# GpSimd adds the 1e-9 to the softmax row sums, and two engines share the last output copy: an attention, gate and bilinear chain on one core

## The chip, the cores and the metric

The kernel runs on one core of a Trainium2 chip. The metric is the device time of one execution in microseconds (us). Engines are named as in the profile: PE is TensorE (PEld its weight loads), DVE is VectorE, ACT is ScalarE, POOL is GpSimd, SP issues the DMAs.

## What is computed

Causal attention over 2 batches, 12 heads, 448 tokens, head size 64, then two dense layers in float32:

```python
scores = np.where(mask, -1e9, (q @ k^T) / sqrt(64))
attn = exp(scores - max); attn = attn / (attn.sum(-1) + 1e-09)
x = (attn @ v) as 896 x 768
h = x @ w_in;  y = (h * cos(h)) @ w_out
out = ((y @ w_a) * (y @ w_b)) @ w_o2
```

## The kernel before

The two heads of a pair lie on the two halves of the 128 partitions, so there are 12 pairs n = 0 to 11. The seven 64-token blocks j of queries of a pair fall into two halves: the even blocks 6, 0, 4, 2 and the odd blocks 5, 3, 1. Below, En and On are the even and the odd half of pair n. For each half the work goes through all engines in turn:

- `scores` (L339): PE multiplies q and k into four PSUM banks.
- `row_max` (L362): DVE adds the mask, takes the row minimum of the negated scores and writes them into one of two buffers p.
- `exps` (L383): ACT takes the exponentials in place and writes each block's row sums into one column of a small tile `sums`, 128x4 for En, 128x3 for On.
- `recip` (L388): DVE adds 1e-9 to that tile (L390) and takes its reciprocal (L391).
- `scale_p` (L398): POOL multiplies the four or three pieces of p by the reciprocals.
- `transposes` (L412): PE transposes seven 128x128 pieces of p into two PSUM banks `pt`, four into the first, three into the second.
- `keep` (L423, L425): one bank is copied to `pp` by ACT, the other by DVE.
- `values` (L439): PE multiplies `pp` and v; `x_hi`, `x_lo` (L449, L454) split the result into a high and a low part.

Every engine runs its instructions strictly in the order in which they were written, and that order is set by hand: a loop over steps i, in each of which the table `CYCLE` is gone through. A pair takes four steps. `(recip, 2, 0)` puts the reciprocal of En at step 4n+2 and `(scale_p, 3, 0)` its scaling at 4n+3; for On they are at 4n+4 and 4n+5. On DVE the next thing behind a `recip` is in most steps a `keep` copy, whose bank the next transposes on PE need.

Beside this, weights are fetched and split into high and low parts (`w_scale`, `w_shift`, `w_pack`, `w_sign`, `w_hi`, `w_lo`); `ASIDE` and `PUMPS` place these by step, behind the entries of `CYCLE`. For the first three chunks both `w_hi` (L129) and `w_lo` (L138) are POOL's; chunk 0 is at step 28, chunk 1 at step 39. From step 44 on, pieces of the first dense layer (L175) fill PE between the attention's parts.

After about 85 us the dense layers follow, with three matmuls per product (high times high, high times low, low times high). At the end each of the 12 output blocks is copied from PSUM by DVE into a tile `o` (L568) and sent off by a DMA from SP's queue (L569).

```python
        CYCLE = [(row_max, 0), (scores, -2), (recip, 2, 0), (recip, 4, 1),
            (keep, 6, 0), (keep, 8, 1), (exps, 0), (scale_p, 3, 0), (scale_p, 5, 1), ...]
```

Of the kernel before, what the change touches and what calls it, by code (L numbers as in the profile page):

```python
# [12 lines left out]
ACTF = mybir.ActivationFunctionType  # L13
ALU = mybir.AluOpType
# [12 lines left out]
def tile_causal_attention_cos_gate_bilinear(  # L27
# [16 lines left out]
    nc = tc.nc  # L44
    B, NPAIR = qk.shape[:2]
    D = P // 2
    S = out.shape[1] // B
    NP = B * NPAIR
    NJ = S // D
    N_IN, N_Y, N_C = w_in.shape[0], w_out.shape[0], w_a.shape[0]  # L50
# [12 lines left out]
    def act_tiles(pool, tag, kind, b, n):  # L63
        return [
            tuple(pool.tile([P, S], F32R, tag=f"{tag}{b}_{t}{part}", name=f"{kind}{b}_{t}{part}") for part in ("hi", "lo"))
            for t in range(n)
        ]
# [73 lines left out]
    def w_pump():  # L141

        i, odd = divmod(next(pumps), 2)
        if odd:
            w_shift(i)
            w_pack(i)
        else:
            w_sign(i - 1)
            w_hi(i - 1)
            w_lo(i - 1, nc.gpsimd)  # L150
            w_scale(i)

    def split(src, pair, lo_engine=None):
        nc.scalar.activation(pair[0], src, ACTF.Copy)
        (lo_engine or nc.vector).tensor_tensor(out=pair[1], in0=src, in1=f32(pair[0]), op=ALU.subtract)
# [10 lines left out]
    def product(kind, f, acts, name, release, parts=1):  # L166

        ps = bank(next(cycle), name)[:, :S]
        n = len(acts)
        t = j = 0  # L170
        while t < n:
            hi, lo, k = chunks[kind, f, j]
            terms = [(hi, c, part) for c in range(k) for part in range(2)] + [(lo, c, 0) for c in range(k)]
            for i, (w, c, part) in enumerate(terms):
                nc.tensor.matmul(  # L175
                    ps,
                    w[:, c * P : (c + 1) * P],
                    acts[t + c][part],
                    start=t == 0 and i == 0,
                    stop=t + k == n and i == len(terms) - 1,  # L180
                )
                if (i + 1) % (len(terms) // parts) == 0 and i + 1 < len(terms):
                    yield ps
            t += k
            if release:
                del chunks[kind, f, j]
            if kind != "in":
                w_pump()
            j += 1
        yield ps  # L190
# [7 lines left out]
    def rows(u):  # L198
        if u < len(units):
            f, b = units[u]  # L200
            stages[u] = next(product("in", f, x[b], "h", b == B - 1))
# [7 lines left out]
    def turns(u):  # L209
        if u in stages:  # L210
            ps = stages[u]
            k = work.tile([P, S], I32, tag="k", name="k", bufs=1)
            r = work.tile([P, S], F32, tag="r", name="r")
            nc.scalar.activation(k, ps, ACTF.Copy, scale=1.0 / TWO_PI)  # L214
            nc.vector.scalar_tensor_tensor(out=r, in0=k, scalar=-TWO_PI, in1=ps, op0=ALU.mult, op1=ALU.add)  # L215
            stages[u] = (ps, r)

    def sine(u):
        if u in stages:
            r = stages[u][1]  # L220
            nc.scalar.activation(r, r, ACTF.Sin, scale=0.5)  # L221

    def square(u):
        if u in stages:
            r = stages[u][1]
            nc.scalar.activation(r, r, ACTF.Square, scale=2.0**0.5)  # L226

    def gate(u):
        if u in stages:
            ps, r = stages[u]  # L230
            nc.vector.scalar_tensor_tensor(out=r, in0=r, scalar=1.0, in1=ps, op0=ALU.subtract, op1=ALU.mult)  # L231

    def g_out(u):
        if u in stages:
            f, b = units[u]
            split(stages.pop(u)[1], g[b][f], nc.gpsimd)
# [23 lines left out]
    P_OFF, o = {}, 0  # L260
# [18 lines left out]
    with ExitStack() as actx:  # L279
# [6 lines left out]
        for o in (0, S):  # L286
            for e in range(2):
                half = mask[e * D : (e + 1) * D, o : o + D]
                nc.gpsimd.affine_select(
                    out=half,  # L290
# [96 lines left out]
        @pairs  # L387
        def recip(n, odd):  # L388
            t = T["sums", n, odd][:, : NB - odd]
            nc.vector.tensor_scalar_add(t, t, 1e-9)  # L390
            nc.vector.reciprocal(t, t)  # L391

        @pairs
# [69 lines left out]
        def at(fn, i):  # L463
# [6 lines left out]
            (row_max, 0),  # L470
            (scores, -2),
            (recip, 2, 0),
            (recip, 4, 1),
            (keep, 6, 0),
            (keep, 8, 1),
# [49 lines left out]
    with tc.manual_schedule():  # L525
        g = [act_tiles(g_pool, "g", "g", b, N_IN) for b in range(B)]
        for u in range(EARLY):
            gate(u - 2)
            turns(u)
            sine(u - 1)  # L530
            g_out(u - 2)
            square(u - 1)
            if u < EARLY - 1:
                w_pump()
        for u in range(EARLY, len(units) + 2):
            gate(u - 2)
            rows(u)
            turns(u)
            sine(u - 1)
            g_out(u - 2)  # L540
            square(u - 1)
            w_pump()


        y = [act_tiles(xy, "xy", "y", b, N_Y) for b in range(B)]
        for m in range(N_Y):
            for b in range(B):
                ps = next(product("out", m, g[b], "y", b == B - 1))
                split(ps, y[b][m])


        c = [act_tiles(g_pool, "g", "c", b, N_C) for b in range(B)]
        for f in range(N_C):
            for b in range(B):
                ps_b = next(product("b", f, y[b], "b", b == B - 1))
                bs = work.tile([P, S], F32, tag="k", name="bs", bufs=1)
                nc.scalar.activation(bs, ps_b, ACTF.Copy)
                ps_a = next(product("a", f, y[b], "a", b == B - 1))
                c32 = work.tile([P, S], F32, tag="r", name="c32")
                nc.vector.tensor_tensor(out=c32, in0=ps_a, in1=bs, op=ALU.mult)  # L560
                split(c32, c[b][f])


        for m in range(N_Y):
            for b in range(B):
                ps = next(product("o2", m, c[b], "o", b == B - 1))
                o = work.tile([P, S], F32, tag="r", name="o")
                nc.vector.tensor_copy(o, ps)  # L568
                nc.sync.dma_start(out=out[m * P : (m + 1) * P, b * S : (b + 1) * S], in_=o)  # L569


# [46 lines left out]
```

## Time and profile before

| | |
|---|---|
| median of 3 runs | 583.26 us (582.53 to 583.45) |
| the profiled execution | 582.98 us, its span 581.2 us |
| PE busy | 572.7 us, 99% of the span |
| DVE, ACT, POOL busy | 360.5, 267.3, 222.7 us |
| granted TensorE clock | 1.0 throughout |

The span runs from the first to the last instruction on the engines; 1.8 us of the profiled execution lie around it. Busy shares are averages over stages with different limits: attention fills the first 85 us of the span and the dense layers the rest. A busy PE is not PE at its peak, since matmuls are pipelined and their ends are modelled.

### The profile page before, as it was taken

How to read it: one execution, taken by the hardware profiler on the slowest of the kernel's cores; microseconds unless marked ns; L12 is line 12 of the kernel's file. 1: busy time of each engine (PE TensorE's matmuls, PEld its weight loads, DVE VectorE, ACT ScalarE, POOL GpSimd, SP SyncE). 2: the span in 40 equal slices, each digit the busy share in tenths (PEclk: the TensorE clock that was granted, in tenths of full speed). 3: DMA queues.
4: the chain of work that ended last, by engine and by line, in shares of the span. 5: the costliest groups of instructions: out<-in, count | busy, mean ns of one | idle time of the engine just before them, and what ended most of it. 6: DMA issues, size and time to landing. Idle time of an engine off the chain costs nothing.

```text
span 581.2 us, 8736 instructions
## 1 busy us (share of the span) xinstructions
PE 572.7 (99%) x3310; PEld 512.1 (88%) x3310; DVE 360.5 (62%) x599; ACT 267.3 (46%) x531; POOL 222.7 (38%) x200
## 2 busy tenths in 40 slices
PE   8999999999999999999999999999999999999997
PEld 6666679999999999999999999999999999999996
DVE  5788856777777775554465666666666666655400
ACT  5877947777777733232223433333333333222100
POOL 4557752666666643232222322222222222322200
PEclk9999999999999999999999999999999999999999
DMA  8745311333332333423243333333323333444000
GB/s 322 264 150 192 109 57 55 109 109 109 109 109 92 108 116 122 144 91 109 91 162 109 110 109 109 108 109 108 110 108 110 110 108 109 140 141 140 33 33 32
DMA packets 15450, 67.80 MB, mean 117 GB/s; under 512 B 1712, under 2 KB 3376, under 8 KB 15408
## 3 DMA queue, kind: packets, MB, share of 16 engines
q1 hardware_dynamic: 15408, 67.25, 34.6%
q8 instruction: 26, 0.43, 0.3%
q14 instruction: 16, 0.13, 0.1%
HBM read 64.49 MB, written 2.75 MB: 116 GB/s over the span
## 4 chain that ended last, share of the span: by engine, by line
PE 93%; DVE 3%; ACT 2%; issue 1%; POOL 0%; DVEq 0%; POOLq 0%
PE h L175 20%; PE y L175 20%; PE o L175 15%; PE a L175 15%; PE b L175 15%; PE xa L439 3%; PE pt L412 2%; ACT p L383 2%; PE s L339 2%; DVE p L362 1%; DVE pp L425 1%; PE warm L459 1%; POOL p L398 0%; DVE sums L390 0%; ACT pp L423 0%
## 5 line engine op out<-in xcount | busy, mean ns | idle before, releaser
L138 POOL TENSOR_TENSOR w_lo<-w_raw,w_hi 128x768 fp32r<-128x768 f32 (+1 forms) x70 | 128.8, 1840 | 264.8 <-ACT w_hi L131 194.1
L111 DVE SCALAR_TENSOR_TENSOR w_raw<-w_raw 128x768 int32<-128x768 int32 (+1 forms) x70 | 124.0, 1772 | 63.2 <-ACT w_raw L100 62.4
L131 ACT ACTIVATE w_hi<-w_raw 128x768 fp32r<-128x768 f32 (+1 forms) x67 | 59.9, 895 | 163.1 <-DVE w_raw L118 100.0
L118 DVE SCALAR_TENSOR_TENSOR w_raw<-w_raw 128x768 int32<-128x768 int32 (+1 forms) x70 | 66.1, 945 | 0.4
L100 ACT ACTIVATE w_raw<-w_raw 128x768 f32<-128x768 f32 (+1 forms) x70 | 61.8, 882 | 0.0
L398 POOL TENSOR_SCALAR p<-p,sums 128x448 f32<-128x448 f32 (+6 forms) x84 | 44.0, 541 | 28.0 <-DVE sums L391 18.5
L383 ACT ACTIVATE p<-p,mn 128x448 f32<-128x448 f32 (+6 forms) x84 | 42.0, 503 | 15.1 <-DVE mn L362 15.1
L105 DVE TENSOR_SCALAR w_raw<-w_raw 128x768 int32<-128x768 int32 (+1 forms) x70 | 42.5, 607 | 0.0
L362 DVE CUSTOM_DVE_ANT_0 p<-s,mask 128x448 f32<-128x448 f32 (+6 forms) x84 | 31.8, 418 | 9.2 <-PE pt L412 4.6
L215 DVE SCALAR_TENSOR_TENSOR r<-k,h 128x448 f32<-128x448 int32 x32 | 19.8, 618 | 26.0 <-ACT k L214 25.7
L568 DVE COPY o<-o 128x448 f32<-128x448 f32 x12 | 7.5, 625 | 35.3 <-PE o L175 35.3
L339 PE MATMUL s<-qk_raw 64*64 64x448 f32 (+6 forms) x336 | 27.4, 395 | 0.3 <-DVE mn L362 0.3
L412 PE MATMUL pt<-ident,p 128*128 128x128 f32 x168 | 23.9, 280 | 3.0 <-ACT pp L423 1.9
L214 ACT ACTIVATE k<-h 128x448 int32<-128x448 f32 x32 | 17.2, 538 | 18.1 <-PE h L175 17.4
L560 DVE TENSOR_TENSOR c<-a,bs 128x448 f32<-128x448 f32 x24 | 15.0, 625 | 15.4 <-PE a L175 15.4
L339 PEld LDWEIGHTS s<-qk_raw 64*64 64x64 f32 x336 | 14.9, 134 | 10.9 <-issue 3.9
L412 PEld LDWEIGHTS pt<-ident,p 128*128 128x128 f32 x168 | 18.1, 140 | 7.0 <-POOL p L398 2.9
L439 PE MATMUL xa<-pp,v 128*64 128x64 f32 (+3 forms) x336 | 23.8, 293 | 0.0
L439 PEld LDWEIGHTS xa<-pp,v 128*64 128x64 f32 x336 | 16.1, 137 | 8.6 <-issue 6.5
L231 DVE SCALAR_TENSOR_TENSOR r<-r,h 128x448 f32<-128x448 f32 x32 | 19.6, 611 | 1.5 <-ACT r L226 1.5
L221 ACT ACTIVATE r<-r 128x448 f32<-128x448 f32 x32 | 18.3, 571 | 0.0
L226 ACT ACTIVATE r<-r 128x448 f32<-128x448 f32 x32 | 18.2, 570 | 0.0
(377 smaller groups left out, 1564.5 us busy)
## 6 DMA issues: line engine op xcount, KB each, us to landing
w_raw<-in_w_in SPq DMA_DIRECT2D x16, 768.0 KB, 4.3
w_raw<-in_w_out SPq DMA_DIRECT2D x12, 768.0 KB, 4.3
w_raw<-in_w_b SPq DMA_DIRECT2D x12, 768.0 KB, 4.3
w_raw<-in_w_a SPq DMA_DIRECT2D x12, 768.0 KB, 4.3
w_raw<-in_w_o SPq DMA_DIRECT2D x12, 768.0 KB, 4.3
v<-in_v SPq DMA_DIRECT2D x12, 448.0 KB, 5.5
qk_raw<-in_qk SPq DMA_DIRECT2D x11, 448.0 KB, 5.5
w_raw<-in_w_out SPq DMA_DIRECT2D x6, 512.0 KB, 3.8
```

The source lines that it names most:

```text
L100: nc.scalar.activation(high, high, ACTF.Copy, scale=2.0**-112)
L105: nc.vector.tensor_single_scalar(low, low, 29, op=ALU.logical_shift_right)
L111: nc.vector.scalar_tensor_tensor(out=low, in0=high, scalar=3, in1=low, op0=ALU.logical_shift_left, op1=ALU.bitwise_or)
L118: nc.vector.scalar_tensor_tensor(out=low, in0=high, scalar=SIGN, in1=low, op0=ALU.bitwise_and, op1=ALU.bitwise_or)
L131: nc.scalar.activation(pair[0][:, :n], src, ACTF.Copy)
L138: engine.tensor_tensor(out=lo[:, :n], in0=f32(raw.pop(i)[:, :, 0]), in1=f32(hi)[:, :n], op=ALU.subtract)
L175: nc.tensor.matmul(ps, w[:, c * P : (c + 1) * P], acts[t + c][part], start=t == 0 and i == 0, stop=t + k == n and i == len(terms) - 1,)
L339: nc.tensor.matmul(T["s", i + c][q, o : o + WIDTH[j]], t[h, Q_COL[j] : Q_COL[j] + D], t[h, FIRST[j] : FIRST[j] + WIDTH[j]], start=True, st ...
L383: nc.scalar.activation(t, t, ACTF.Exp, bias=T["mn", n][:, c], scale=-1.0, accum_out=row_sum(n, j))
L398: nc.gpsimd.tensor_scalar(out=t, in0=t, scalar1=row_sum(n, j), scalar2=1.0, op0=ALU.mult, op1=ALU.mult)
L412: nc.tensor.transpose(dst, p_bufs[n % N_P][:, o : o + P], ident)
L439: nc.tensor.matmul(ps[e * D : (e + 1) * D, o * D : w * D], t[:, k, e], p[:, :, :, q].rearrange("p s l q -> p (s l) q") if k < 3 else p[:, ...
```

## The change

The addition of 1e-9 goes from DVE to POOL; the reciprocal stays on DVE. Of the 12 output copies the last is cut in two: DVE copies the first 224 columns, ACT the other 224.

```diff
         def recip(n, odd):
             t = T["sums", n, odd][:, : NB - odd]
-            nc.vector.tensor_scalar_add(t, t, 1e-9)
+            nc.gpsimd.tensor_scalar(out=t, in0=t, scalar1=1e-9, scalar2=1.0, op0=ALU.add, op1=ALU.mult)
             nc.vector.reciprocal(t, t)
...
-                nc.vector.tensor_copy(o, ps)
+                if (m, b) < (N_Y - 1, B - 1):
+                    nc.vector.tensor_copy(o, ps)
+                else:
+                    nc.vector.tensor_copy(o[:, : S // 2], ps[:, : S // 2])
+                    nc.scalar.activation(o[:, S // 2 :], ps[:, S // 2 :], ACTF.Copy)
```

The order of POOL's instructions around weight chunk 1 (step 39) and behind it, as a difference of the two programs; L390 is the addition, p_116 and p_115 are the two p buffers, and the first L390 shown belongs to O9, the second to E10:

```order
 L129 TENSOR_SCALAR w_hi<-w_raw 128x768
 L138 TENSOR_TENSOR w_lo<-w_raw,w_hi 128x768
+L390 TENSOR_SCALAR sums<-sums 128x3
 L398 TENSOR_SCALAR p_116<-p_116,sums 128x384
 L398 TENSOR_SCALAR p_116<-p_116,sums 128x256
 L398 TENSOR_SCALAR p_116<-p_116,sums 128x128
+L390 TENSOR_SCALAR sums<-sums 128x4
 L398 TENSOR_SCALAR p_115<-p_115,sums 128x448
```

Each addition now stands in POOL's queue directly ahead of the scaling of its own half, and so behind the scaling of the half before; O9's stands behind w_hi and w_lo of weight chunk 1 as well. At chunk 0 (step 28) it is the other way round: O6's addition stands ahead of w_hi and w_lo, O6's scaling and E7's addition behind them.

The same place, O9, on DVE before (each row with the engines on which its instruction waits):

```order
L362 ISA p_115,mn<-s,mask 128x64 [waits PE_49,Pool_49]
L362 ISA mn 128x1
L390 TENSOR_SCALAR sums<-sums 128x3 [waits Activation_49]
L391 RECIPROCAL sums<-sums 128x3 [waits DVE_49]
L425 COPY pp<-pt 128x3x128
L362 ISA p_115,mn<-s,mask 128x320 [waits Pool_49]
```

and now:

```order
L362 ISA p_115,mn<-s,mask 128x64 [waits PE_49]
L362 ISA mn 128x1
L391 RECIPROCAL sums<-sums 128x3 [waits Pool_49]
L425 COPY pp<-pt 128x3x128
L362 ISA p_115,mn<-s,mask 128x320
```

The first instruction of `recip` on DVE waited for ACT's sums before; now the reciprocal waits for POOL, and the copy and the row minima behind it in DVE's queue wait with it.

The end of the program on ACT, before:

```order
L131 ACTIVATE w_hi<-w_raw 128x768 [waits DVE_49,PE_49]
L100 ACTIVATE w_raw<-w_raw 128x768 [waits DMAHW3_49,Pool_49]
L131 ACTIVATE w_hi<-w_raw 128x768 [waits DVE_49,PE_49]
L612 UNCONDITIONAL_BRANCH
```

and now (L572 is ACT's half of the last copy):

```order
L131 ACTIVATE w_hi<-w_raw 128x768 [waits DVE_49,PE_49]
L100 ACTIVATE w_raw<-w_raw 128x768 [waits DMAHW3_49,Pool_49]
L131 ACTIVATE w_hi<-w_raw 128x768 [waits DVE_49,PE_49]
L572 ACTIVATE o<-o 128x224 [waits DMAHW6_49,DMAHW0_49,DVE_49]
L616 UNCONDITIONAL_BRANCH
```

ACT's half of the copy names DVE among its waits and not PE, whose product it reads; the DVE count that it waits for is that of DVE's own half of the copy, the last instruction that DVE has.

## Rows read from the trace of the kernel before

**Rows 1.** The page's section 4: the chain that ended last, by engine.
```profile
PE 93%; DVE 3%; ACT 2%; issue 1%; POOL 0%; DVEq 0%; POOLq 0%
```
**Rows 2.** Two stretches: busy us (instructions) of PE, PEld, DVE, ACT, POOL; clock, DMA.
```profile
17.00:35.00 18.00, 18.00 (x224) 12.54 (x218) 13.88 (x63) 15.62 (x53) 9.69 (x21) 1.00 0.72 240
35.00:48.00 13.00, 11.96 (x134) 7.68 (x134) 12.21 (x44) 9.97 (x35) 9.67 (x14) 1.00 0.20 64
```
**Rows 3.** Line L390: ns min/median/max of one, first and last start in us.
```profile
L390 DVE TENSOR_SCALAR sums<-sums x24: 163/170/582, 8.7 to 77.4; 128x4 f32<-128x4 f32 x12, 128x3 f32<-128x3 f32 x12
```
**Rows 4.** POOL by form (17 to 35 us; last row: start): busy us, mean ns | idle.
```profile
L398 POOL TENSOR_SCALAR p<-p,sums 128x448 f32<-128x448 f32 x3 | 1.9, 639 | 3.3 <-DVE sums L391 3.3
...
L398 POOL TENSOR_SCALAR p<-p,sums 128x64 f32<-128x64 f32 x3 | 0.9, 317 | 0.0
...
L606 POOL MEMSET const-float32-0.0<- 128x1 f32 x1 | 0.1, 99 | 0.2 <-issue 0.2
```
**Rows 5.** Timeline at E5: start us, us, instruction [idle before <-releaser].
```profile
35.19 0.21 ACT L383 ACTIVATION_READ_ACCUMULATOR p<-p,mn 128x1 f32 x1
35.42 0.17 DVE L390 TENSOR_SCALAR sums<-sums 128x4 f32<-128x4 f32 x1 [0.72 <-ACT p L383]
```
**Rows 6.** The chain that ended last, pieces in order of time: start us, us, what.
```profile
8.69 0.18 DVE sums L390
...
45.08 0.07 issue
...
61.84 0.09 DVE sums L390
```
**Rows 7.** Timeline at E0 and O0, start of the program: DVE, POOL, PE.
```profile
8.89 0.18 DVE L391 RECIPROCAL sums<-sums 128x4 f32<-128x4 f32 x1
...
9.29 3.23 POOL L398 TENSOR_SCALAR p<-p,sums 128x448 f32<-128x448 f32 x7 [6.70 <-ACT p L383]
...
10.45 0.30 DVE L390 TENSOR_SCALAR sums<-sums 128x3 f32<-128x3 f32 x1 [0.16 <-ACT p L383]
...
15.46 0.95 PE L412 MATMUL pt<-ident,p 128*128 128x128 f32 x7 [0.52 <-ACT pp L423]
```
**Rows 8.** Timeline around weight chunk 0 (O6, E7, O7) and after: POOL, DVE, ACT, PE.
```profile
45.05 0.89 POOL L129 TENSOR_SCALAR w_hi<-w_raw 128x768 fp32r<-128x768 f32 x1
...
47.85 3.21 POOL L398 TENSOR_SCALAR p<-p,sums 128x384 f32<-128x384 f32 x7
...
45.38 0.58 DVE L390 TENSOR_SCALAR sums<-sums 128x3 f32<-128x3 f32 x1
...
48.60 0.66 DVE L425 COPY pp<-pt 128x512 f32<-128x512 f32 x1
...
50.96 0.60 ACT L423 ACTIVATE pp<-pt 128x512 f32<-128x512 f32 x1 [0.34 <-PE pt L412]
...
59.43 0.95 PE L412 MATMUL pt<-ident,p 128*128 128x128 f32 x7 [0.52 <-ACT pp L423]
```
**Rows 9.** Timeline around weight chunk 1 (O9): DVE, POOL, PE.
```profile
64.73 0.22 DVE L390 TENSOR_SCALAR sums<-sums 128x3 f32<-128x3 f32 x1
...
65.08 0.53 DVE L425 COPY pp<-pt 128x384 f32<-128x384 f32 x1
...
65.88 1.86 POOL L138 TENSOR_TENSOR w_lo<-w_raw,w_hi 128x768 fp32r<-128x768 f32 x1
67.72 3.20 POOL L398 TENSOR_SCALAR p<-p,sums 128x384 f32<-128x384 f32 x7
...
65.52 0.96 PE L412 MATMUL pt<-ident,p 128*128 128x128 f32 x7 [0.40 <-ACT pp L423]
```
**Rows 10.** The last copy (timeline); lines L425 and L423: ns min/median/max, starts, forms.
```profile
577.09 0.62 DVE L568 COPY o<-o 128x448 f32<-128x448 f32 x1 [6.67 <-PE o L175]
...
L425 DVE COPY pp<-pt x24: 527/609/685, 12.8 to 83.1; 128x512 f32<-128x512 f32 x12, 128x384 f32<-128x384 f32 x12
...
L423 ACT ACTIVATE pp<-pt x24: 467/532/600, 12.4 to 82.8; 128x384 f32<-128x384 f32 x12, 128x512 f32<-128x512 f32 x12
```

## Prediction, made before the changed kernel had run

> **What bounds the kernel now.** I read the chain of waits first. By engine it is 93% PE, and only 3% DVE and 2% ACT [rows 1]. In the dense layers PE is a wall that neither edit touches, until the last copy. So I read attention alone, by stretches. From 17 to 35 us PE is busy 18.00 of 18.00 us while DVE is busy 13.88: there DVE may be a little late at no cost. From 35 to 48 us PE has 11.96 of 13.00 and DVE 12.21, because the first weight chunk's shifts and packs have joined the softmax on DVE [rows 2]. The reader is to see that in this second stretch, and up to about 62 us, DVE, ACT and PE pass the bound among them, and that a wait put into DVE's queue has little to hide in. The pieces of the chain say the same: it goes through L390 nine times, first at 8.69 and last at 61.84 us [rows 6]. From there on PE has filler work and no idle time worth the name, so what attention loses before then is added to the end.
>
> **The addition on GpSimd: the price of one.** DVE is freed of 24 additions of about 0.17 us [rows 3], some 4 us in all. But the reciprocal needs the sum, so the way from ACT to the reciprocal gets longer. Before: ACT's last sum is there at 35.40, the addition starts 0.02 us later, takes 0.17, and the reciprocal follows about 0.03 after it [rows 5]: 0.22. After: a hop from ACT to POOL, the addition there, a hop back. No row has a POOL addition on four columns. Its scalings take 0.317 us at 64 columns and 0.639 at 448, so 0.84 ns per column and 0.26 us at none: 0.27 for ours. The ends are the 0.10 us of a one-column memset below and the 0.32 of the 64 columns above [rows 4]; I stay on the line, since the operation is the same. The hop back is 0.07, as POOL to DVE shows at 45.08 [rows 6]. The hop to POOL lies between the 0.02 of ACT to DVE [rows 5] and the 0.22 from the end of a reciprocal at 9.07 to POOL's start at 9.29 [rows 7]; I take the middle, 0.12. Together 0.46, so each passage is 0.24 longer, call it 0.22 with roundings.
>
> Of the nine passages of the chain I leave out one, which falls into the stretch where PE is always busy [rows 2], and O7's, which is counted with E7 below. Seven are left: 7 x 0.22 = 1.5 us. From that comes a gain: O6's addition took 0.58 us instead of 0.17 [rows 3, 8], since it ran beside w_hi on POOL and ended with it (45.96 against 45.94). Without it 0.4 is saved. **Net 1.1 us.**
>
> [...]
>
> **The addition on GpSimd: its queue.** POOL works in order, so an addition also waits for what stands ahead of it. In the even run of attention POOL has finished the previous scaling by then. In three places it has not.
>
> - O0. E0's scaling starts at 9.29, and its four pieces last until about 11.13 (1.84 by the line of rows 4: 0.26 x 4 + 0.84 x 1024 columns gives 1.9). O0's addition is then over at 11.40 instead of 10.75 [rows 7]. DVE's next row minima, ACT's exponentials of E1 and the copy behind them move by that, down to the transposes at 15.46, which waited for ACT's copy already [rows 7]. **0.65 us.**
> - O6 and E7, weight chunk 0. O6's addition stands ahead of w_hi and cannot start before the sums at 45.38 [rows 8], so w_hi, which started at 45.05, now starts at 45.65, and O6's scaling at 48.45 instead of 47.85. Its three pieces take 1.4 by the line of rows 4, and only then comes E7's addition: over at 50.1, reciprocal at 50.2, the copy behind it at 50.3 instead of 48.60. DVE is 1.7 us late. On ACT 0.34 of that falls into a wait it had anyway at 50.96 [rows 8]; the other 1.35 reach E8's exponentials, whose sums DVE then needs, with another 0.2 for E8's own passage, and come out at 59.43, where PE waits for ACT's copy [rows 8]. **1.55 us.**
> - O9, weight chunk 1. Here the addition stands behind w_hi and w_lo. Before, DVE adds at 64.73 and copies at 65.08, while POOL is in w_lo until 67.72 [rows 9]. Now the addition runs 67.72 to 67.99, the reciprocal starts at 68.05, the copy at 68.15 and ends at 68.68. PE's transposes at 65.52 write two banks: four pieces go at once, until about 66.07, and the last three need the bank that this copy frees. They start at 68.75. **2.7 us** of PE standing still, where before its wait was the 0.40 ahead of 65.52. What POOL and DVE then owe (scaling of O9, E10) ends before PE comes to it, since PE is late by as much.
>
> **The last copy.** DVE's 448 columns take 0.62 us. By the copies of 384 and 512 columns, 0.53 and 0.66 to 0.69, half of it is 0.37 on DVE; on ACT (0.47 and 0.60) 0.33 [rows 10]. Side by side this would save 0.2. But the order of the program shows ACT's half waiting for DVE's count and not for PE's, so the halves run one behind the other: 0.37 + 0.02 + 0.33 = 0.72, and a first instruction of ACT after a long pause. **0.15 us** slower, at the very end, uncovered.
>
> [...]
>
> **Sum.** 1.1 + 0.65 + 1.55 + 2.7 + 0.15 = 6.15, so 582.98 + 6.2 = **589.2 us**. The profiled execution lies 0.3 under the median of the three runs, which is nothing against the terms; on the median it would be 589.5.
>
> The bounds: twelve additions stand in the sum (seven, O0, O6, E7, E8, O9). At 0.10 us each it is 2.0 lower, at 0.32 0.6 higher; the hop to POOL moves nine of them by 0.1 either way, 0.9. The way from E7 to PE is the longest and may lose its half to idle time that I did not see, 0.8. So 585.6 at one end; at the other 590.7, and to about 592.3 if PE has to wait behind O9 a second time, for E10, by as much as E7's 1.55.
>
> **Rivals.**
>
> - *The waits are hidden.* VectorE only reaches a reciprocal when it is due, and PE has other work. For it: 18 us without PE idle [rows 2]. Against: at O9 the row order is fixed, transposes behind the copy behind the reciprocal, and PE has no filler before step 44. If it held, only the 0.15 of the end is left: 583.1.
> - *Faster: VectorE is freed.* The chain's nine passages each hold an addition of at least 0.17 us, 1.5 in all, and O6's holds 0.4 more [rows 3, 6, 8]. This decides if POOL's addition with both hops costs under 0.22 us and the queue is empty: then 583.0 - 1.9 + 0.15 = 581.2. Against: 0.46 by the rows, and POOL's queue is visibly full at O9. [...]
> - *A small POOL instruction is dear.* If its fixed cost, which no row at four columns shows, were near 1 us instead of 0.27, twelve times 0.7 come on top: 597.6. Against: 0.10 and 0.32 on either side [rows 4].
> - *The halves do overlap at the end.* Changes 0.35 us and no sign.
>
> **How the numbers follow.** My case has 0.85: the three queue places follow from the order alone. Hidden has 0.05, faster 0.04, the dear instruction 0.06. A measurement of this kernel can tell about 0.2%, 1.2 us, from no change. So faster 0.04, same 0.05, slower 0.91. The range for 8 in 10 holds my case with its bounds, 585.6 to 592.3; the others stay outside.
>
> **What would show it.** Right: a DVE idle time ahead of L391, released by POOL L390, of over 3 us once (O9) and about 1.7 once (E7), and a PE wait of 2 to 3 us ahead of three transposes near 70 us of the new span; POOL's addition at 0.2 to 0.3 us; ACT's L572 starting when DVE's L571 ends; the dense layers unchanged in length, only shifted. Wrong: attention's end shifted by under 2 us, or PE's waits spread evenly over all 24 passages (then the price of one is off, not the queue), or additions of 0.5 us and more.

## The result, and the profile after

The changed kernel takes **588.1 us** (median of 5 executions, 587.71 to 591.23) where the one before takes 583.36; the two medians stand at 1.0081, and the ratio over all executions is 1.0105, 95% interval [1.009, 1.012]. So it is slower, by 4.7 us where 6.2 were forecast. The profiled execution takes 587.91 us. Three of the five executions are at 587.7 to 588.1, two at 590.9 and 591.2 with a mean TensorE clock of 0.994 instead of 0.998 or more, which raise the ratio; experiments 8 to 10 take that up, and the rest compares the three.

The chain that ended last, by engine. POOL, which had 0% of it before [rows 1], has 2%:

```profile
PE 91%; ACT 3%; DVE 2%; POOL 2%; issue 1%; POOLq 0%; DVEq 0%
```

The lines L390 and L391, and the waits (engine and line, what released it: us in total, times, longest us):

```profile
L390 POOL TENSOR_SCALAR sums<-sums x24: 194/196/199, 8.5 to 82.0; 128x4 f32<-128x4 f32 x12, 128x3 f32<-128x3 f32 x12
...
DVE sums L391 <- POOL sums L390: 15.5, 20, 3.2
```

An addition on POOL takes 0.196 us, against 0.170 on DVE [rows 3], and the reciprocal waits for it 20 times of 24, 15.5 us in all. That sum is no loss yet: the loss is read where the wait goes on to PE. First E0 and O0 (ACT's last sum of E0, then DVE, then POOL; start us, us, instruction, in brackets the idle time before it and its releaser):

```profile
8.11 0.19 ACT L383 ACTIVATION_READ_ACCUMULATOR p<-p,mn 128x1 f32 x1
```
```profile
8.70 0.18 DVE L391 RECIPROCAL sums<-sums 128x4 f32<-128x4 f32 x1 [1.20 <-POOL sums L390]
...
11.13 0.17 DVE L391 RECIPROCAL sums<-sums 128x3 f32<-128x3 f32 x1 [1.04 <-POOL sums L390]
```
```profile
8.47 0.19 POOL L390 TENSOR_SCALAR sums<-sums 128x4 f32<-128x4 f32 x1 [5.88 <-ACT p L383]
8.97 1.84 POOL L398 TENSOR_SCALAR p<-p,sums 128x448 f32<-128x448 f32 x4 [0.31 <-DVE sums L391]
10.90 0.20 POOL L390 TENSOR_SCALAR sums<-sums 128x3 f32<-128x3 f32 x1
```

O0's addition has no idle time before it: it starts when E0's scaling is over, and DVE idles 1.04 us for it. Then E7 behind weight chunk 0 (POOL, DVE, PE):

```profile
50.52 0.19 POOL L390 TENSOR_SCALAR sums<-sums 128x4 f32<-128x4 f32 x1
...
50.75 0.18 DVE L391 RECIPROCAL sums<-sums 128x4 f32<-128x4 f32 x1 [1.96 <-POOL sums L390]
...
51.55 0.55 PE L412 MATMUL pt<-ident,p 128*128 128x128 f32 x3 [0.41 <-DVE pp L425]
```

And O9 behind weight chunk 1, in order of time:

```profile
67.74 1.84 POOL L138 TENSOR_TENSOR w_lo<-w_raw,w_hi 128x768 fp32r<-128x768 f32 x1
...
69.67 0.20 POOL L390 TENSOR_SCALAR sums<-sums 128x3 f32<-128x3 f32 x1
69.90 0.17 DVE L391 RECIPROCAL sums<-sums 128x3 f32<-128x3 f32 x1 [3.23 <-POOL sums L390]
69.99 0.53 DVE L425 COPY pp<-pt 128x384 f32<-128x384 f32 x1
...
70.67 0.52 PE L412 MATMUL pt<-ident,p 128*128 128x128 f32 x3 [2.67 <-DVE pp L425]
```

One stop can be followed through four engines here: w_lo holds POOL until 69.6, the addition of three columns stands behind it, DVE's reciprocal waits 3.23 us, the copy stands behind the reciprocal, and TensorE stands still for 2.67 us ahead of the last three of E9's seven transpositions. Before, all seven went in one run, and the only wait was the 0.40 ahead of the first [rows 9].

The end of the program (DVE, ACT, SP):

```profile
581.71 0.39 DVE L571 COPY o<-o 128x224 f32<-128x224 f32 x1 [6.67 <-PE o L175]
...
582.14 0.36 ACT L572 ACTIVATE o<-o 128x224 f32<-128x224 f32 x1 [27.13 <-DVE o L571]
...
582.52 0.33 SPq L573 DMA_DIRECT2D out_t<-o  x1
```

The halves run one behind the other. From the copy's start to the DMA it takes 0.81 us; before, the copy began at 577.09 [rows 10] and the DMA's row reads:

```profile
577.74 0.33 SPq L569 DMA_DIRECT2D out_t<-o  x1
```

That was 0.65, so the divided copy costs 0.16. From that DMA's issue to the end of the span it takes 3.59 us, before 3.43; why, no run shows (with the divided copy alone, experiment 1, it is 3.42).

**A ruler for the rest.** The first row minimum on DVE starts when PE's first scores are there. It is at 5.90 us in the trace before, at 5.56 after, and between 5.46 and 6.46 in the others, so positions are compared from there. The end of attention is the last start of L439 (values), which its line gives to 0.1 us. Before, then after:

```profile
5.90 0.63 DVE L362 CUSTOM_DVE_ANT_0 p<-s,mask 128x448 f32<-128x448 f32 x1 [4.50 <-PE s L339]
...
L439 PE MATMUL xa<-pp,v x336: 219/222/537, 17.4 to 88.4; 128*64 128x64 f32 x96, 128*64 128x384 f32 x24, 128*64 128x256 f32 x24, 128*64 128x128 f32 x24
```
```profile
5.56 0.62 DVE L362 CUSTOM_DVE_ANT_0 p<-s,mask 128x448 f32<-128x448 f32 x1 [4.16 <-PE s L339]
...
L439 PE MATMUL xa<-pp,v x336: 219/222/537, 17.9 to 93.0; 128*64 128x64 f32 x96, 128*64 128x384 f32 x24, 128*64 128x256 f32 x24, 128*64 128x128 f32 x24
```

88.4 - 5.9 = 82.5 us before and 93.0 - 5.6 = 87.4 after: **attention is 4.9 us longer**. From there to the start of the last copy it is 488.7 us in both (577.09 - 88.4 and 581.71 - 93.0), so the dense layers are only shifted. The span grew by 4.9 as well, 586.1 against 581.2, since attention began 0.3 us earlier in it and the two differences at the end add 0.3.

### The profile page after: what moved, and what is told of

The parts are those of the page before. It is cut to its first block, busy times and chain, and to the rows that moved or that the text cites. A ratio compares the mean times of both kernels' runs of the same rounds, so it can differ in the third digit from the quotient of the medians.

```text
span 586.1 us, 8728 instructions
## 1 busy us (share of the span) xinstructions
PE 573.4 (98%) x3310; PEld 512.5 (87%) x3310; DVE 355.3 (61%) x575; ACT 267.4 (46%) x532; POOL 228.2 (39%) x224
## 4 chain that ended last, share of the span: by engine, by line
PE 91%; ACT 3%; DVE 2%; POOL 2%; issue 1%; POOLq 0%; DVEq 0%
PE h L175 20%; PE y L175 20%; PE o L175 15%; PE a L175 15%; PE b L175 15%; ACT p L383 3%; PE xa L439 2%; PE pt L412 2%; PE s L339 1%; DVE pp L425 1%; POOL w_lo L138 1%; POOL p L398 1%; DVE p L362 1%; PE warm L459 1%; POOL sums L390 0%
## 5 line engine op out<-in xcount | busy, mean ns | idle before, releaser
L412 PE MATMUL pt<-ident,p 128*128 128x128 f32 x168 | 24.1, 280 | 6.5 <-DVE pp L425 3.1
L412 PEld LDWEIGHTS pt<-ident,p 128*128 128x128 f32 x168 | 18.1, 140 | 10.9 <-POOL sums L390 3.9
L439 PE MATMUL xa<-pp,v 128*64 128x64 f32 (+3 forms) x336 | 23.8, 293 | 0.0
L439 PEld LDWEIGHTS xa<-pp,v 128*64 128x64 f32 x336 | 16.1, 137 | 8.5 <-issue 6.5
```

Source lines behind the costliest of these rows:

```text
L412: nc.tensor.transpose(dst, p_bufs[n % N_P][:, o : o + P], ident)
L439: nc.tensor.matmul(ps[e * D : (e + 1) * D, o * D : w * D], t[:, k, e], p[:, :, :, q].rearrange("p s l q -> p (s l) q") if k < 3 else p[:, ...
```

## The experiments

The theory: the loss is made in POOL's queue at three places (O0, E7, O9) and at the end; a passage through POOL by itself costs little. Rival A: the longer way over POOL costs something at each of the 24 passages. Rival B: the divided copy costs more than its rows show. "Attention" below is the length by the ruler, against the 82.5 us before.

| | what differs from the changed kernel | us (before, same chip) | ratio, interval | attention |
|---|---|---|---|---|
| 1 | all additions back on DVE | 583.3 (583.01) | 1.0002 [0.9993, 1.0012] | 0.0 |
| 2 | O9's addition on DVE | 586.32 (583.01) | 1.0055 [1.0043, 1.0068] | +3.2 |
| 3 | O0's, E7's, O9's on DVE | 584.41 (583.01) | 1.0023 [1.0014, 1.0031] | +1.0 |
| 4 | as 3, and E10 to O11 on DVE; last copy whole | 582.93 (582.71) | 1.0003 [0.9994, 1.0012] | 0.0 |
| 5 | O9's addition ahead of w_hi and w_lo | 586.94 (583.01) | 1.0067 [1.0055, 1.008] | +3.7 |
| 6 | only pairs 2 to 4 on POOL; last copy whole | 582.64 (582.71) | 0.9999 [0.999, 1.0008] | -0.4 |
| 7 | no addition at all; last copy whole | 581.17 (582.71) | 0.997 [0.9959, 0.9982] | -2.0 |
| 8 | nothing | 590.74 (582.71) | 1.0136 [1.0122, 1.015] | |
| 9 | TensorE's stop at O9 filled | 588.79 (583.07) | 1.01 [1.0085, 1.0115] | +5.0 |
| 10 | nothing | 589.05 (583.07) | 1.0106 [1.0083, 1.0128] | +6.2 |

**1. The divided copy alone.**

```diff
-            nc.gpsimd.tensor_scalar(out=t, in0=t, scalar1=1e-9, scalar2=1.0, op0=ALU.add, op1=ALU.mult)
+            nc.vector.tensor_scalar_add(t, t, 1e-9)
```

> Only the shared last copy; all 24 additions are back on VectorE. Queue theory (the loss is made in attention, at the places where GpSimd's queue is not free when an addition is due): attention as before, and at the end ScalarE's half starts only when VectorE's half is over, so the last DMA is issued about 0.15 us later than before: 583.5. Rival (the halves overlap, the order of the program tells nothing of it): ScalarE's half starts with VectorE's and the time is 583.1. Second rival (a good part of the 4.7 us is made at the end, by ScalarE starting after a long pause): 585 or more.

583.3 against 583.01 us: no difference that can be measured, and at most 0.7 us (0.12% of 583). The 0.16 of the rows fits in there. Rival B is out, and the loss is the addition's.

**2 and 3. The places of the queue.** The same two instructions with a condition, here that of 3:

```diff
-            nc.gpsimd.tensor_scalar(out=t, in0=t, scalar1=1e-9, scalar2=1.0, op0=ALU.add, op1=ALU.mult)
+            if (n, odd) in ((0, 1), (7, 0), (9, 1)):
+                nc.vector.tensor_scalar_add(t, t, 1e-9)
+            else:
+                nc.gpsimd.tensor_scalar(out=t, in0=t, scalar1=1e-9, scalar2=1.0, op0=ALU.add, op1=ALU.mult)
```

> The changed kernel, but the one addition of the odd half of pair 9 (the one behind the second weight chunk in GpSimd's queue) is on VectorE again; 23 stay on GpSimd. Queue theory: the idle time of TensorE of 2.7 us at that place goes, nothing else changes: 588.1 - 2.8 = 585.3. Rival (each of the 24 passages costs about the same, 4.7 / 24 = 0.2 us, by the longer way through GpSimd): 587.9.

> The changed kernel, but the three additions that the prediction found behind other work in GpSimd's queue (odd half of pair 0, even half of pair 7, odd half of pair 9) are on VectorE again; 21 stay on GpSimd. Queue theory: 588.1 less 2.8 (pair 9), less 1.3 (pair 7 and what follows it on ScalarE), less 0.3 (pair 0) = 583.7, near the kernel before. Rival (even cost per passage): 588.1 - 3 x 0.2 = 587.5.

Between 2 and 3 lie O0 and E7: attention 3.2 against 1.0, so 2.2 us, where 0.65 + 1.55 = 2.2 were forecast. By the ruler the two places can be told apart: O1's transpositions start 0.62 us later in 2 than in 3 (20.16 - 5.88 against 19.71 - 6.05), E8's 2.20 later (61.55 - 5.88 against 59.52 - 6.05). In 2 the stop at O9 is gone, yet the kernel is 1.0 us slower than expected. The trace shows where that went (DVE, then POOL and PE, of experiment 2; its lines are shifted by 3):

```profile
71.54 0.18 DVE L394 RECIPROCAL sums<-sums 128x4 f32<-128x4 f32 x1 [1.46 <-POOL sums L393]
```
```profile
69.86 1.38 POOL L401 TENSOR_SCALAR p<-p,sums 128x384 f32<-128x384 f32 x3
71.32 0.19 POOL L393 TENSOR_SCALAR sums<-sums 128x4 f32<-128x4 f32 x1
...
72.35 0.55 PE L415 MATMUL pt<-ident,p 128*128 128x128 f32 x3 [0.19 <-DVE pp L428]
...
81.22 0.95 PE L415 MATMUL pt<-ident,p 128*128 128x128 f32 x7 [0.58 <-ACT pp L426]
```

O9's scaling still stands behind w_lo (69.86), and E10's addition behind that scaling: DVE waits 1.46 us there instead, and PE pays at 72.35 and 81.22. In the changed kernel this wait is covered, since PE is late at O9 already. So it is a next bottleneck that only shows when the first is taken away, and 3 has it too.

**4. The queue avoided.** The condition is that of 3 with `or n > 9`, so 17 additions stay on POOL.

> The additions of the odd half of pair 0, the even half of pair 7, the odd half of pair 9 and all four of pairs 10 and 11 are on VectorE, the other 17 on GpSimd; the last copy is whole again. Queue theory: with the three blocked places back on VectorE the remaining 1.0 us of loss sits behind the second weight chunk (pairs 10 and 11), and goes too; what is left is the gain of 0.35 us by 35 us: 582.7. Rival (17 passages at 0.2 us each, evenly): 586.

582.93 against 582.71 us, and attention as long as before. Seventeen passages over POOL, those of pairs 5 to 8 among them, cost together nothing that can be seen, where rival A said 586. That settles it. But this is a sum of both signs: the six of pairs 2 to 4 gain 0.4 (experiment 6), so the other eleven cost about 0.4. E10's wait is gone with it: 1.0 us of attention less than in 3.

**5. Another order at O9.** The addition stays on POOL but is issued at step 39 ahead of the chunk:

```diff
-            nc.gpsimd.tensor_scalar(out=t, in0=t, scalar1=1e-9, scalar2=1.0, op0=ALU.add, op1=ALU.mult)
+            if (n, odd) != (9, 1):
+                nc.gpsimd.tensor_scalar(out=t, in0=t, scalar1=1e-9, scalar2=1.0, op0=ALU.add, op1=ALU.mult)
...
+                if i == 39:
+                    t = T["sums", 9, 1][:, : NB - 1]
+                    nc.gpsimd.tensor_scalar(out=t, in0=t, scalar1=1e-9, scalar2=1.0, op0=ALU.add, op1=ALU.mult)
                 for step, fn, *args in ASIDE:
```

> The changed kernel, but the addition of the odd half of pair 9 is issued at the end of step 39, ahead of the second weight chunk's two GpSimd instructions instead of behind them; all 24 stay on GpSimd, and their number, length and hops are the same. Queue theory: VectorE is no longer held for 3.2 us there; GpSimd's two weight instructions now hold the next addition (even half of pair 10), of which about 0.9 us comes through to TensorE: 588.1 - 2.7 + 0.9 = 586.3. Rival (even cost per passage, the place in the queue does not matter): 588.1.

DVE waits for the addition only 0.34 us, but POOL's scalings behind the chunk are later still (70.72 against 69.86 in 2), and PE again pays at E10 and O11, 0.42 and 0.57 us. The place in the queue decides, not the engine; but moving the one instruction forward gives back only 1.2 us of the 4.9.

**6. The stretch in which PE reads as always busy.** Pairs 2 to 4 alone on POOL.

> Six of the 24 additions, those of pairs 2 to 4 (17 to 35 us), are on GpSimd, the other 18 on VectorE; the last copy is whole again. Theory of the hidden gain: in this stretch GpSimd's queue is free, and the step from VectorE's addition to the copy that frees a bank for TensorE was the limit although TensorE read as busy, so each pair takes 5.57 us instead of 5.76 and the kernel gains about 0.55 us: 582.5. Rival (the prediction's own reading: TensorE is busy 18.00 of 18.00 us there, so nothing can be gained): 583.0, a pair takes 5.76 us.

By time it can't be told from no change (the interval reaches from -0.1 to +0.08%). The trace does tell it. PE's transpositions of the same half in two successive pairs, before, after, and in this kernel (where L412 is L415):

```profile
19.35 0.99 PE L412 MATMUL pt<-ident,p 128*128 128x128 f32 x7
...
25.11 0.98 PE L412 MATMUL pt<-ident,p 128*128 128x128 f32 x7
```
```profile
19.85 0.98 PE L412 MATMUL pt<-ident,p 128*128 128x128 f32 x7
...
25.42 0.99 PE L412 MATMUL pt<-ident,p 128*128 128x128 f32 x7
```
```profile
19.87 0.99 PE L415 MATMUL pt<-ident,p 128*128 128x128 f32 x7
...
25.45 0.98 PE L415 MATMUL pt<-ident,p 128*128 128x128 f32 x7
```

A pair takes 5.76 us before and 5.57 and 5.58 with the addition on POOL, 0.19 less, about what one addition with its gap takes in DVE's queue. Before, O3's sums were there at 25.42, and DVE came to the addition at 26.39, 0.97 late and with no idle time ahead of it; in this kernel POOL adds at 26.22, and DVE's reciprocal follows at 26.62, again with no idle time. So DVE's queue set the pace in a stretch where PE reads 18.00 of 18.00 us busy: the move *gains* there, 0.19 us a pair, of which 0.4 is left at the end of attention. PE's share hides it, since the same 16 score matmuls stretch over 1.23 us before and 1.09 in this kernel and read as busy throughout:

```profile
27.80 1.23 PE L339 MATMUL s<-qk_raw 64*64 64x448 f32 x16
```
```profile
28.09 1.09 PE L339 MATMUL s<-qk_raw 64*64 64x448 f32 x16
```

**7. What the additions are worth.** Left out in this kernel is the 1e-9: the row sums are at least 1, where a float32 step is about 1e-7, so the addition changes no digit of them.

```diff
-            nc.gpsimd.tensor_scalar(out=t, in0=t, scalar1=1e-9, scalar2=1.0, op0=ALU.add, op1=ALU.mult)
```

> The addition of 1e-9 is left out (no engine does it); the last copy is whole again. The sums are at least 1, where 1e-9 is less than half of a float32 step. If VectorE's part is worth something (the prediction's rival in which it is faster, 0.2 us on each of the chain's nine passages, and 0.4 more beside the first weight chunk): 0.55 us in 17 to 35 us, and some 1.4 us more after that: 581.0. If the addition lay hidden: 583.0. This is also the ceiling of what moving it to any other engine can bring.

581.17 us: faster than both kernels, by 1.5 and 6.9 us, and attention 2.0 shorter than before. The length is the better measure, since the executions start at different points. That is the whole prize a cheaper addition could win; the forecast's faster rival, 1.9, would have needed nearly all of it.

**8 to 10. The second level of the times.** The changed kernel again, and with the fourth of E9's transpositions repeated:

```diff
-                nc.tensor.transpose(dst, p_bufs[n % N_P][:, o : o + P], ident)
+                for _ in range(18 if (n, odd, c) == (9, 0, 3) else 1):
+                    nc.tensor.transpose(dst, p_bufs[n % N_P][:, o : o + P], ident)
```

> The changed kernel again, unchanged, beside the others on the same chip. 588.1 as before. Two of its five runs took 590.9 and 591.2 at a mean granted clock of 0.994 instead of 0.999; if that comes from its longest stop of TensorE, some of these runs show it again, and no run of the kernels without that stop does. If it is chance, it may turn up in any kernel or not at all.

> The changed kernel with one of E9's transpositions, the fourth of seven, done 18 times instead of once. It stands just ahead of the three pieces that wait at O9, and writes the same numbers each time, so it fills about 2.3 of the 2.67 us in which TensorE stood still there (17 more at 0.135 us), and nothing waits for it. The stop's length stays, so the work behind it starts where it did. Theory (the stop itself makes the granted clock fall behind it in some executions, which then take 590 to 591 us): every execution of this kernel is at 587.5 to 588.5 us with a mean clock of 0.998 or more, none at 590, and the median is 588.0. Rival (the falls of the clock are a matter of the chip and the moment, not of the stop): executions at 590 to 591 us come here too, about as often as in the unchanged copy of the same call.

> The changed kernel itself, unchanged, beside the one with the filled stop, on the same chip. Theory: some or most of its executions at 590 to 591 us with a mean clock near 0.994, so a median between 588.1 and 590.7 us. Rival: the same mixture of times in both kernels.

Run again, the unchanged copy gave four executions at 590.1 to 591.4 (8; 588.1 was expected), then three at 587.7 to 588.0 and three at 590.1 to 591.6 (10). In all, 6 of 15 executions of it are at 587.7 to 588.1 with a mean clock of 0.998 or more, and 9 at 590.1 to 591.6 with 0.994 to 0.996. With the stop filled all four are at 588.78 to 588.80, clock 0.999 or more; that is 0.8 above what was expected, as its first row minimum comes 0.9 us later than in the profiled execution that the expectation was made from (6.43 against 5.56), with attention as long. The stretches behind the stop in 10, and then in 9 (us, busy us of PE, PEld, DVE, ACT, POOL with instructions; granted clock, DMA):

```profile
68.00:70.00 2.00, 0.63 (x4) 0.42 (x4) 0.00 (x0) 1.53 (x6) 1.92 (x2) 1.00 0.00 0
70.00:72.00 2.00, 0.46 (x3) 0.49 (x3) 1.23 (x7) 0.17 (x1) 1.60 (x4) 0.84 0.26 55
72.00:74.00 2.00, 2.00 (x17) 1.09 (x17) 1.84 (x8) 1.90 (x7) 1.05 (x4) 0.50 0.97 351
74.00:76.00 2.00, 2.00 (x27) 1.21 (x22) 1.10 (x7) 0.99 (x4) 1.61 (x5) 0.80 0.56 224
```
```profile
68.00:70.00 2.00, 1.75 (x16) 1.78 (x17) 0.00 (x0) 1.52 (x6) 1.92 (x2) 1.00 0.00 0
70.00:72.00 2.00, 1.17 (x10) 0.80 (x8) 1.20 (x5) 0.14 (x1) 1.60 (x4) 1.00 0.29 65
72.00:74.00 2.00, 2.00 (x23) 1.20 (x24) 1.84 (x8) 1.92 (x7) 1.04 (x4) 1.00 0.94 356
```

In 10 the clock falls behind a stop of 2.65 us: it is below 1.0 in all three windows from 70 to 76 us, and at 0.50 in the middle one; PE does 17 instructions in the 2 us where it does 23 in 9. Both traces start alike (the first row minimum at 6.46 and 6.43 us), so attention's 6.2 against 5.0 is the price of the fall, 1.3 us before rounding; by the times it is 1.4 there (590.14 against 588.78), and 2.8 in the slowest execution if that started as late. Before the change, and in experiments 1 to 7, where PE's longest wait behind the first row minimum is 0.67 us, no execution has a mean clock under 0.998. So filling the stop kept the clock at 0.999 or more in all four executions: the theory holds, and chance alone doesn't explain the second level.

## Why the prediction was right, and where it was not

The direction, the mechanism and the order of the queue's terms were right; the sum was 1.1 us too large against the three executions at 588, by one term. (Two things that it didn't have, the earlier start of attention in the profiled execution and the later end of its span, are 0.3 and 0.17 us and of opposite sign.)

- *O0, 0.65, and O6 with E7, 1.55.* Together 2.2, measured 2.2, of which 0.62 is there by O1 (experiments 2 and 3). O0's addition stands behind E0's scaling, E7's behind O6's, as said; DVE's wait at E7 was 1.96 us, forecast about 1.7.
- *O9, 2.7.* PE's stop is 2.67 us; 4.9 in all less 2.2 for the other places and 0.0 for the passages (experiment 4) leaves 2.7. Putting this one addition back gives only 1.8, because the stop had covered the wait at E10 and O11 (experiment 2).
- *The last copy, 0.15.* 0.16 by the rows; too small for experiment 1 to tell. The rival in which the halves overlap is out: ACT's half starts 0.04 us after DVE's ends. Why it waits, beyond the order of the program, no run shows.
- *The longer passages, net 1.1: this term failed.* Experiment 4 measures 0.0 for 17 of them. Two things were wrong in it. The price: a POOL addition takes 0.196 us and not 0.27, since a line through 64 and 448 columns does not reach down to four. From ACT's last sum to the reciprocal the first passage takes 0.40 us (8.11 + 0.19 = 8.30 to 8.70), the other six of the forecast's seven (E1, E5, O5, E6, O6, E9) 0.31 to 0.39; before, they took 0.24 to 0.65, O6's the longest. Added up, the seven with O6's gain are 0.3 us longer, and experiments 4 and 6 leave 0.4 for the eleven outside pairs 2 to 4. And the step "there DVE may be a little late at no cost", from PE's 18.00 of 18.00 us: nothing was counted there, while DVE was the limit and the move gains 0.19 us a pair, 0.4 at the end of attention (experiment 6). 0.4 less 0.4 is the 0.0.
- *Where that reading went astray.* In the same row of the windows PE's weight loads are busy 12.54 of 18.00 us, 70% [rows 2]. Matmuls that are stretched out still read as busy: the same 16 for 1.23 us before and 1.09 in experiment 6. PE's busy time said 100% in this stretch, and 3% of the pair's time was won there (0.19 of 5.76 us); whether the weight loads' share is a better measure, one stretch does not show.
- *The rival "VectorE is freed"* holds in pairs 2 to 4, where DVE was late and POOL free, for 0.4 us, and is lost elsewhere. *Hidden* and *a small POOL instruction is dear* are out: the waits reach PE, and the price is 0.196 us.

What stays open: which executions lose the clock. The stop is as long in the one that keeps it (2.67 us) as in the two traces that don't (2.64 and 2.65); these two start 0.9 us later. By their times none of the six that keep it starts as late as those of experiment 9 (588.8), so a late start may go with the loss; these runs can't tell.

## What to carry to other kernels

Before an instruction is moved to an idle engine, look at what stands ahead of it in that engine's queue at each place where it is issued, and at what stands behind the one that waits for it: here 17 of 24 moves came out at nothing together, three cost 3.9 us of the 4.9 and four more the rest once those were gone, and a mean busy share of 38% on POOL told nothing of it. A PE that reads 100% busy need not be the bound: here it read 18.00 of 18.00 us where a pair's period went from 5.76 to 5.57 us. Compare the periods of a loop before calling a stretch covered. And the best version was neither engine's: the addition that changes no digit can go, for 1.5 us by the times and 2.0 of attention.

## What the runs showed of the hardware that was not expected

A stop of TensorE of 2.6 to 2.7 us can cost more than itself: in 9 of 15 executions the mean clock is lower, in the two of these that were profiled it was below 1.0 in three windows of 2 us and 0.50 in the middle one, and in the one that can be compared with the filled stop the time rose by 1.4 us. Filling the stop with work that nothing needs removed this in all four executions (clock 0.999 or more, 588.78 to 588.80 us). POOL's additions on three and four columns all take 0.194 to 0.199 us, though its 64 columns take 0.317 [rows 4]; where its queue is free, POOL starts 0.09 to 0.17 us after ACT's last sum (0.17 from 8.30 to 8.47; before, DVE started 0.02 to 0.03 after it), and where DVE waits for it, its reciprocal starts 0.03 to 0.04 after POOL's end (8.66 to 8.70).
